# V loaded in two-token runs and put in order by TensorE, with merged final stores and new priorities, in a linear-attention and token-mixing kernel

## The chip, the cores and the metric

The kernel runs on one core of a Trainium2 chip. The metric is the device time of one execution in microseconds (us). Each comparison lists a median; the fast runs of one kernel are those within 1.5% of its fastest, and the others are called slow. Ratios are the mean time of one kernel's fast runs over that of the other's fast runs of the same rounds, so they are not quite the ratios of the medians.

The engines are TensorE (PE in the profile, its weight loads PEld), VectorE (DVE), ScalarE (ACT), GpSimd (POOL) and the sync engine (SP), which here only issues transfers. SPq is its queue.

## The reference

Four batch entries, 8 heads, 768 tokens, head width 48. First a recurrence per head, then a token mixer over the joined heads (384 columns):

```python
for t in range(S):
    cur = einsum('bhd,bhe->bhde', u * k_t, v_t)
    y[:, :, t] = einsum('bhd,bhde->bhe', r_t, state + cur)
    state = w_t[..., None] * state + einsum('bhd,bhe->bhde', k_t, v_t)
x = y joined over heads                                   # B, S, 384
wq, wk = x @ w_q, x @ w_k                                 # width 64
W_tok = scale * einsum('bsd,btd->bst', wq, wk)
out = relu(einsum('bst,btd->bsd', W_tok, x)) @ w_out
```

The recurrence runs in chunks of 128 tokens: decays become exponentials of summed logarithms, and each chunk needs a masked 128 by 128 product per head and one update of the state. Two chunks make a unit; there are 12 units, three to a batch entry. The token mixer of an entry can only end after its third unit, so its six stores come in a lump at each batch change.

## The kernel before

W, K and R are loaded with two neighbouring tokens on each partition, so a run in memory is 2 x 48 fp32 = 384 B. V is wanted in another order, the even tokens of a chunk on partitions 0 to 63 and the odd ones on 64 to 127, and it is loaded straight into that order, in four issues with runs of 192 B:

```python
def load(b, i, tl, ap):
    nc.sync.dma_start(out=view(tl, 0, [[D2, H], [1, D2]]),
        in_=ap[b, :, ds(i * U, U)].rearrange("h (p j) d -> p h (j d)", j=2))

def load_v(b, i, tl, c):                       # called for c = 0 and 1
    src = v[b, :, ds(i * U + c * C, C)].rearrange("h (q j) d -> j q h d", j=2)
    for j in range(2):
        nc.sync.dma_start(out=view(tl, c * DM, [[D, H], [1, D]], p0=64 * j, pn=64),
                          in_=src[j])
...
def f_vb():                                    # GpSimd, fp32 to bf16
    nc.gpsimd.tensor_copy(sb("VB", [C, 2 * DM]), vg)
...
def f_st(ii=ii, osb=osb, cs=cs):               # stores, two for each step
    dst = out[b, ds(ii * U, U)].rearrange("(c q j) d -> j q c d", j=2, q=64)
    for j in range(2):
        nc.sync.dma_start(out=dst[j][:, ds(cs[0], len(cs))], in_=view(osb, ...))
```

The order of instructions on each engine is fixed when the program is built. A small list scheduler takes the steps with their estimated lengths, a priority (`STEP * n + OFF[...]` for unit `n`) and the free buffers, and emits the steps in the order in which it would start them. Loads and stores share one queue, in that order; a store that waits for its data at the head of the queue holds all loads behind it. Inputs have three buffers each, and PSUM is handed out bank by bank.

## Time and profile before

| | before |
|---|---|
| the first three timed runs | 127.17, 127.18, 129.46 us |
| span of the profiled run (125.04 us) | 123.3 us |
| TensorE busy | 96.1 us, 78% |
| VectorE, GpSimd, ScalarE busy | 84.6, 77.4, 75.6 us |
| ScalarE's logarithm waiting for W | 10.1 us |

How to read the profile's lines: `wg`, `kg`, `rg` and `vg` are the buffers in which W, K, R and V land, `lw` is the logarithm, `os` the output buffer, `AM` a mask product; L374 is a line of the kernel. In rows of 40 digits the span is cut into 40 equal slices (numbered from 0), and a digit is the busy share of a slice in tenths, 9 being 90% or more. PEclk is the clock granted to TensorE, in tenths of full speed. DMA is the mean busy share of the 16 DMA engines; the windows give it as a fraction that can come out above 1.

The profile's row for that logarithm (busy us and mean ns of one, then the idle time of the engine before it and its cause):

```profile
L374 ACT ACTIVATE lw<-wg 128x768 bf16<-128x768 f32 x12 | 10.1, 844 | 10.1 <-DMA wg<-in_w_dram 10.1
```

Every unit starts with it: ScalarE waited 10.1 us in all for W to land.

### The profile page before, as it was taken

The page shows a single profiled execution, that of the slowest core. Times are in us where ns is not written, and L with a number is a line of the kernel's source. Part 1 is how long each engine was busy: PE and PEld are TensorE (multiplying, and loading weights), DVE is VectorE, ACT ScalarE, POOL GpSimd, SP SyncE. Part 2 cuts the span into 40 slices and gives each one's busy share as a digit, 9 for nine tenths or more (in the row PEclk, how much of TensorE's full clock was granted, in tenths as well). Part 3 has the DMA queues.
Part 4 walks back from the last instruction along what each step waited for, and adds up shares of the span by engine and source line. Part 5 has one row for each costly group of instructions (what it writes and reads, how often), then busy time and mean ns, then how long its engine had stood idle before and what let it go on. Part 6 is the DMA issues. An engine that isn't in the chain of part 4 may idle for free.

```text
span 123.3 us, 3766 instructions
## 1 busy us (share of the span) xinstructions
PE 96.1 (78%) x1528; PEld 71.7 (58%) x1528; DVE 84.6 (69%) x139; ACT 75.6 (61%) x105; POOL 77.4 (63%) x96
## 2 busy tenths in 40 slices
PE   0268986969699999679699998596999998969600
PEld 0256865847577678458477587484676885634300
DVE  6627969768685869682688998665975989634500
ACT  4362454659759958567667698487599894336100
POOL 6379699898895937943996848669945575200000
PEclk9999999999999999967999999999999999995875
DMA  3999989996999979999979688989899760000663
GB/s 67 307 224 312 189 255 299 203 308 125 266 227 229 275 167 254 262 227 222 275 159 312 117 223 241 297 155 312 177 273 248 197 196 0 0 0 5 158 152 73
DMA packets 67968, 24.62 MB, mean 200 GB/s; under 512 B 64496, under 2 KB 67952, under 8 KB 67952
## 3 DMA queue, kind: packets, MB, share of 16 engines
q1 hardware_dynamic: 67536, 24.39, 80.9%
q8 instruction: 12, 0.20, 0.6%
q10 hardware_dynamic: 416, 0.00, 0.2%
q14 instruction: 4, 0.03, 0.1%
HBM read 19.66 MB, written 4.72 MB: 198 GB/s over the span
## 4 chain that ended last, share of the span: by engine, by line
PE 33%; SPq 18%; ACT 14%; DMA 12%; POOL 9%; issue 6%; DVE 3%; ACTq 0%; POOLq 0%
PE PS L161 33%; POOL KT L447 8%; DMA wg<-in_w_dram 8%; SPq L197 7%; SPq L204 7%; ACT ep L406 5%; ACT en L400 5%; DMA vg<-in_v_dram 3%; SPq L718 2%; ACT lw L374 1%; ACT XT L297 1%; DVE os L301 1%; POOL ptm L453 1%; ACT QK L297 1%; SPq L727 1%
## 5 line engine op out<-in xcount | busy, mean ns | idle before, releaser
L496 DVE TENSOR_TENSOR AM<-PS,US 128x1024 bf16<-128x1024 f32 x24 | 28.8, 1218 | 3.4 <-PE PS L161 3.3
L447 POOL TENSOR_TENSOR KT<-ks,en 128x1024 bf16<-128x1024 bf16 (+1 forms) x13 | 23.7, 1824 | 4.6 <-DVE ks L425 2.4
L478 POOL TENSOR_TENSOR Vd<-VB,dd 128x768 bf16<-128x768 bf16 (+1 forms) x14 | 18.0, 1291 | 4.9 <-DVE dd L473 4.5
L400 ACT ACTIVATE en<-PS 128x1024 bf16<-128x1024 f32 (+1 forms) x14 | 12.6, 902 | 9.3 <-PE PS L161 7.2
L374 ACT ACTIVATE lw<-wg 128x768 bf16<-128x768 f32 x12 | 10.1, 844 | 10.1 <-DMA wg<-in_w_dram 10.1
L161 PE MATMUL PS<-CM,lw 64*128 64x128 bf16 x192 | 8.7, 240 | 7.5 <-ACT lw L374 7.3
L425 DVE COPY ks<-PS 128x1024 bf16<-128x1024 bf16 x12 | 8.3, 690 | 9.0 <-PE PS L161 9.0
L161 PE MATMUL PS<-wo,MX 128*128 128x384 bf16 x72 | 14.0, 356 | 0.2 <-ACT MX L307 0.2
L161 PEld LDWEIGHTS <-KT 48*128 48x128 bf16 (+1 forms) x272 | 10.6, 98 | 6.2 <-POOL KT L447 3.3
L297 ACT COPY XT<-PS 128x768 bf16<-128x768 bf16 (+1 forms) x12 | 9.2, 768 | 6.7 <-PE PS L161 6.7
L542 DVE TENSOR_TENSOR SB<-PS,ptm 128x384 bf16<-128x384 f32 x20 | 11.1, 553 | 2.7 <-PE PS L161 2.5
L406 ACT ACTIVATE ep<-PS 128x1024 bf16<-128x1024 f32 (+1 forms) x14 | 12.9, 919 | 0.0
L381 POOL CAST k<-kg 128x768 bf16<-128x768 f32 x12 | 9.9, 822 | 4.3 <-DMA kg<-in_k_dram 4.2
L381 POOL CAST r<-rg 128x768 bf16<-128x768 f32 x12 | 9.9, 826 | 3.8 <-DMA rg<-in_r_dram 3.8
L461 POOL CAST VB<-vg 128x768 bf16<-128x768 f32 x12 | 9.9, 824 | 3.7 <-PE PS L161 3.7
L299 ACT ACTIVATE X<-PS,gx 128x768 bf16<-128x768 f32 (+1 forms) x11 | 9.6, 870 | 4.0 <-PE PS L161 3.1
L161 PEld LDWEIGHTS <-lw 64*128 64x128 bf16 x192 | 6.5, 105 | 8.7 <-ACT lw L374 7.7
L436 DVE TENSOR_TENSOR RT<-PS,ep 128x1024 bf16<-128x1024 bf16 (+1 forms) x14 | 8.5, 612 | 3.5 <-PE PS L161 3.5
L161 PEld LDWEIGHTS <-MX 128*128 128x128 bf16 x72 | 7.3, 105 | 5.7 <-issue 1.6
L161 PE MATMUL PS<-RT,KT 48*128 48x128 bf16 x192 | 8.8, 225 | 1.6 <-POOL KT L447 1.0
L161 PEld LDWEIGHTS <-AM 128*128 128x128 bf16 x192 | 8.7, 99 | 2.0 <-issue 0.3
L301 DVE COPY os<-PS 128x768 f32<-128x768 f32 (+1 forms) x7 | 5.5, 786 | 5.6 <-PE PS L161 4.0
(70 smaller groups left out, 197.1 us busy)
## 6 DMA issues: line engine op xcount, KB each, us to landing
wg<-in_w_dram SPq DMA_DIRECT2D x12, 384.0 KB, 4.1
kg<-in_k_dram SPq DMA_DIRECT2D x12, 384.0 KB, 5.1
rg<-in_r_dram SPq DMA_DIRECT2D x12, 384.0 KB, 6.1
vg<-in_v_dram SPq DMA_DIRECT2D x48, 96.0 KB, 4.0
out_dram<-os SPq DMA_DIRECT2D x18, 192.0 KB, 3.0
out_dram<-os SPq DMA_DIRECT2D x12, 96.0 KB, 2.2
wof<-in_moe_w_out_dram SPq DMA_DIRECT2D x1, 576.0 KB, 4.9
wqf<-in_moe_w_q_dram SPq DMA_DIRECT2D x1, 96.0 KB, 4.0
```

Source lines behind the costliest of these rows:

```text
L161: nc.tensor.matmul(o, l, rr, start=start, stop=stop, skip_group_check=True, is_transpose=trans)
L297: nc.scalar.copy(o, i)
L299: nc.scalar.activation(o, i, ACT.Copy, bias=0.0, scale=by)
L374: nc.scalar.activation(view(lw, 0, [[64, H], [512, 2], [1, D]]), view(wg, 0, [[D2, H], [D, 2], [1, D]]), ACT.Ln, bias=0.0, scale=math.exp( ...
L381: nc.gpsimd.tensor_copy(view(dst, 0, [[64, H], [512, 2], [1, D]]), view(src, 0, [[D2, H], [D, 2], [1, D]]))
L400: nc.scalar.activation(sb("en", [C, 1024])[:, cols(cs, 512)], t["cw"][:, cols(cs, 512)], ACT.Exp, bias=0.0, scale=-1.0)
L406: nc.scalar.activation(view(ep, cs[0] * NP * EW + 66, [[EW, NP * len(cs)], [-65, 2], [1, 64]]), t["cw"][:, cols(cs, 512)], ACT.Exp, bias=0 ...
L447: e.tensor_tensor(sb("KT", [C, 1024])[:, cols(cs, 512)], t["ks"][:, cols(cs, 512)], t["en"][:, cols(cs, 512)], ALU.mult)
L461: nc.gpsimd.tensor_copy(sb("VB", [C, 2 * DM]), vg)
L478: nc.gpsimd.tensor_tensor(sb("Vd", [C, 2 * DM])[:, cols(cs, DM)], t["VB"][:, cols(cs, DM)], view(t["dd"], cs[0] * H, [[1, len(cs) * H], [0 ...
L496: nc.vector.tensor_tensor(view(sb(f"AM{c}", [C, 1024]), 0, [[C, 8], [1, C]]), view(t[f"A{c}"], 0, [[C, 8], [1, C]]), view(US, 0, [[0, 8], ...
L542: nc.vector.tensor_tensor(view(x, 0, [[D, H], [1, D]]), view(t[f"sn{c}"], 0, [[D, H], [1, D]]), view(t["ptm"], c * 8, [[1, 8], [0, D]]), A ...
```

## The change

The intent is fewer and longer transfers. V is loaded like K, in one issue of 384 B runs. GpSimd casts it, TensorE puts the tokens in order by products with a 0/1 selection matrix, and ScalarE or VectorE copies the result out of PSUM. Merged final stores and new priorities come with it. The core of the diff, shortened:

```diff
+    PM = const([C, 2 * C], BF16, "PM")                    # 0/1, built at the start
-    OFF = dict(load=-4, ln=207, c16=-50, ...)
-    ENG = dict(KT="PPPPPPPPPPDP", kd="DDADADDADDAD", ...)
+    OFF = dict(load=-38, ln=232, c16=-17, ..., v16=-147, vp=-43, vb=-59, ...)
+    ENG = dict(KT="PPPPPPPPPDPP", vb="AAAADAADAAAA", kd="DDADDAADADAA", ...)
...                                                         # and new cost estimates
-        add("SP", 2150, "load", f_lv, fill="vg", ...)       # 4 issues
+        add("SP", 1500, "load", lambda: load(b, i, vg, v), fill="vg", ...)
...
-            nc.gpsimd.tensor_copy(sb("VB", [C, 2 * DM]), vg)
+            nc.gpsimd.tensor_copy(view(v16, 0, [[D, H], [DM, 2], [1, D]]),
+                                  view(vg, 0, [[D2, H], [D, 2], [1, D]]))
+        def f_vp():
+            t["vp"] = x = wtile("vp")                       # two PSUM banks
+            for j in range(2):
+                for c in range(2):
+                    mm(x[:, ds(c * 512, DM)], PM[ds(c * 64, 64), ds(j * C, C)],
+                       v16[ds(c * 64, 64), ds(j * DM, DM)], start=(j == 0), stop=(j == 1))
+        def f_vb():
+            copy(vbe, VB, vp)                               # ScalarE 10x, VectorE 2x
...
-  last batch: f_st for each half unit, two issues of 96 KB each, all on sync (12)
+  last batch: f_st for each unit, two issues of 192 KB (6), the very last on ScalarE's queue
...
+  the last token sum's copies wait for all of its groups, not for the last alone
```

More of the change, by code (lines that the diff above doesn't have):

```diff
@@ L199, in load @@
             in_=ap[b, :, ds(i * U, U)].rearrange("h (p j) d -> p h (j d)", j=2))
-    def load_v(b, i, tl, c):
-        src = v[b, :, ds(i * U + c * C, C)].rearrange("h (q j) d -> j q h d", j=2)
-        for j in range(2):
-            nc.sync.dma_start(out=view(tl, c * DM, [[D, H], [1, D]], p0=64 * j, pn=64),
-                              in_=src[j])
     ID16 = const([C, C], BF16, "ID16")
@@ L225 @@
     nc.vector.memset(ID16, 0.0)
+    nc.vector.memset(PM, 0.0)
     for t in LW:
@@ L247 @@
                                     fill=0.0, base=-j, channel_multiplier=-2)
+    for c in range(2):
+        for j in range(2):
+            m = PM[ds(c * 64, 64), ds(j * C + j * 64, 64)]
+            nc.gpsimd.affine_select(m, m, pattern=[[1, 64]], compare_op=ALU.not_equal,
+                                    fill=1.0, base=0, channel_multiplier=-1)
     nc.gpsimd.affine_select(ID16, ID16, pattern=[[1, C]], compare_op=ALU.not_equal, fill=1.0,
@@ L258 @@
     STEP = 100
-    OFF = dict(load=-4, ln=207, c16=-50, cw=60, ex=34, rT=123, ks=-72, qT=284, RT=139, KT=27,
-               ptm=275, vb=34, dps=61, vd=-63, A=8, am=115, kb=94, kd=-148, sn=-109, sb=184,
-               y=108, x=-84, xt=129, xts=-98, qk=64, qks=249, T=148, mx=-51, rl=317, fp=103,
-               os=13, st=149)
-    ENG = dict(KT="PPPPPPPPPPDP", kd="DDADADDADDAD", xts="AAAAAAAAAAAD", x="AAADAAAAAAAA",
-               qks="DAAAAAAAAADA", rl="AAAADAAAAAAA", os="AADDDAADADAD")
+    OFF = dict(load=-38, ln=232, c16=-17, cw=-165, ex=-1247, rT=520, ks=698, qT=-1585, RT=735,
+               KT=49, ptm=-98, v16=-147, vp=-43, vb=-59, dps=288, vd=-159, A=-391, am=545,
+               kb=332, kd=-769, sn=-476, sb=170, y=86, x=-436, xt=541, xts=-163, qk=811,
+               qks=-869, T=612, mx=226, rl=-553, fp=-948, os=1147, st=189)
+    ENG = dict(KT="PPPPPPPPPDPP", vb="AAAADAADAAAA", kd="DDADDAADADAA", xts="DADAAAADDDAA",
+               x="AAAAAAAAAAAA", qks="DAADAAADAADA", rl="DDDAAAAAAAAA", os="AAADAAAADAAD")
     SPLIT = (0, B * NU - 1)
@@ L272 @@
         kinds[name] = 2
-    for name in ("en", "ks", "qT", "RT", "KT", "ptm", "VB", "dd", "Vd", "AM0", "AM1", "KD", "XT"):
+    for name in ("en", "ks", "qT", "RT", "KT", "ptm", "v16", "VB", "dd", "Vd", "AM0", "AM1", "KD", "XT"):
         kinds[name] = NS
@@ L290, in took @@
         if eng == "P":
-            return 60 + int(cols * 1.87)
-        return 110 + int(cols * (0.52 if half else 1.04))
+            return 100 + int(cols * 1.93)
+        return 150 + int(cols * (0.52 if half else 1.04))
     def copy(eng, o, i, by=None):
@@ L360, in cols @@
             return ds(cs[0] * w_, len(cs) * w_)
-        g = {x: Got() for x in ("wg kg rg vg lw k16 r16 cw ep en kT rT ks qT RT KT ptm VB dps dd Vd"
+        g = {x: Got() for x in ("wg kg rg vg lw k16 r16 v16 vp cw ep en kT rT ks qT RT KT ptm VB dps dd Vd"
                                 " A0 A1 AM0 AM1 kb KD sn y xt XT qk").split()}
-        add("SP", 1460, "load", lambda: load(b, i, wg, w), fill="wg", got=g["wg"], lag=2000)
-        add("SP", 1460, "load", lambda: load(b, i, kg, k), fill="kg", got=g["kg"], lag=2000)
-        add("SP", 1460, "load", lambda: load(b, i, rg, r), fill="rg", got=g["rg"], lag=2000)
-        def f_lv():
-            load_v(b, i, vg, 0)
-            load_v(b, i, vg, 1)
-        add("SP", 2150, "load", f_lv, fill="vg", got=g["vg"], lag=2000)
+        add("SP", 1500, "load", lambda: load(b, i, wg, w), fill="wg", got=g["wg"], lag=2000)
+        add("SP", 1500, "load", lambda: load(b, i, kg, k), fill="kg", got=g["kg"], lag=2000)
+        add("SP", 1500, "load", lambda: load(b, i, rg, r), fill="rg", got=g["rg"], lag=2000)
+        add("SP", 1500, "load", lambda: load(b, i, vg, v), fill="vg", got=g["vg"], lag=2000)
         def f_ln():
@@ L425, in f_ks @@
             nc.vector.tensor_copy(sb("ks", [C, 1024]), t["kT"])
-        add("D", 640, "ks", f_ks, fill="ks", got=g["ks"], use=[g["kT"]])
+        add("D", 670, "ks", f_ks, fill="ks", got=g["ks"], use=[g["kT"]])
         def f_qT():
             nc.vector.tensor_tensor(sb("qT", [C, 1024]), t["rT"], t["ks"], ALU.mult)
-        add("D", 640, "qT", f_qT, fill="qT", got=g["qT"], use=[g["rT"], g["ks"]])
+        add("D", 670, "qT", f_qT, fill="qT", got=g["qT"], use=[g["rT"], g["ks"]])
         for cs in fine:
@@ L458, in unit, with f_v16 @@
                 use=[g["ep"]])
+        def f_v16():
+            nc.gpsimd.tensor_copy(view(sb("v16", [C, 2 * DM]), 0, [[D, H], [DM, 2], [1, D]]),
+                                  view(vg, 0, [[D2, H], [D, 2], [1, D]]))
+        add("P", 830, "v16", f_v16, fill="v16", got=g["v16"], use=[g["vg"]])
+        def f_vp():
+            t["vp"] = x = wtile("vp")
+            for j in range(2):
+                for c in range(2):
+                    mm(x[:, ds(c * 512, DM)], PM[ds(c * 64, 64), ds(j * C, C)],
+                       t["v16"][ds(c * 64, 64), ds(j * DM, DM)], start=(j == 0), stop=(j == 1))
+        add("PE", 370, "vp", f_vp, fill="w", got=g["vp"], use=[g["v16"]])
+        vbe = ENG["vb"][n]
         def f_vb():
-            nc.gpsimd.tensor_copy(sb("VB", [C, 2 * DM]), vg)
-        add("P", 830, "vb", f_vb, fill="VB", got=g["VB"], use=[g["vg"]])
+            copy(vbe, view(sb("VB", [C, 2 * DM]), 0, [[DM, 2], [1, DM]]),
+                 view(t["vp"], 0, [[512, 2], [1, DM]]))
+        add(vbe, took(vbe, 2 * DM), "vb", f_vb, fill="VB", got=g["VB"], use=[g["vp"]])
         def f_dps():
@@ L499, in f_am @@
                     view(US, 0, [[0, 8], [1, C]]), ALU.mult)
-            add("D", 1180, "am", f_am, more=2 * c, fill=f"AM{c}", got=g[f"AM{c}"], cs=(c,),
+            add("D", 1200, "am", f_am, more=2 * c, fill=f"AM{c}", got=g[f"AM{c}"], cs=(c,),
                 use=[g[f"A{c}"]])
@@ L544, in f_sb @@
                                             view(t["ptm"], c * 8, [[1, 8], [0, D]]), ALU.mult)
-                st_ = add("D", 510, "sb", f_sb, more=2 * c, fill="SB", cs=(c,), use=[gsn, g["ptm"]])
+                st_ = add("D", 540, "sb", f_sb, more=2 * c, fill="SB", cs=(c,), use=[gsn, g["ptm"]])
                 new.put(st_, (0, 1))
@@ L646, in unit @@
         groups = [[0, 1, 2, 3], [4], [5]] if end else [list(range(NCH))]
+        Tall = []
         for gs in groups:
-            T_ = add("PE", 165 * len(gs), "T", f_T(gs),
+            Tall.append(add("PE", 165 * len(gs), "T", f_T(gs),
                      [batch["qks"][x] for x in gs] + [batch["xs"][x] for x in gs]
                      + ([gT.first] if gT.first else []),
-                     more=OFF["am"] - OFF["T"] if end and gs[0] == 0 else 0, fill="s", got=gT)
+                     more=OFF["am"] - OFF["T"] if end and gs[0] == 0 else 0, fill="s", got=gT))
         def f_Ts(c):
@@ L662, in f_Ts @@
             return f
-        Ts = [add("AD"[c], took("AD"[c], DM), "T", f_Ts(c), [T_], more=1, use=[gT])
+        Ts = [add("AD"[c], took("AD"[c], DM), "T", f_Ts(c), Tall, more=1, use=[gT])
               for c in range(2 if end else 1)]
@@ L713, in unit, with f_st, f @@
                     use=[gf])
-                def f_st(ii=ii, osb=osb, cs=cs):
+            def f_st(j, e, ii=ii, osb=osb):
+                def f():
                     dst = out[b, ds(ii * U, U)].rearrange("(c q j) d -> j q c d", j=2, q=64)
-                    for j in range(2):
-                        nc.sync.dma_start(
-                            out=dst[j][:, ds(cs[0], len(cs))],
-                            in_=view(osb, cs[0] * DM, [[DM, len(cs)], [1, DM]], p0=64 * j, pn=64))
-                add("SP", 560 * len(cs), "st", f_st, more=6 * ii, cs=cs, use=[go], lag=2000)
+                    e.dma_start(out=dst[j],
+                                in_=view(osb, 0, [[DM, 2], [1, DM]], p0=64 * j, pn=64))
+                return f
+            add("SP", 620, "st", f_st(0, nc.sync), more=6 * ii, use=[go], lag=2000)
+            if end and ii == NU - 1:
+                add("A", 500, "st", f_st(1, nc.scalar), more=6 * ii, use=[go], lag=2000)
+            else:
+                add("SP", 620, "st", f_st(1, nc.sync), more=6 * ii, use=[go], lag=2000)
     state = {}
```

## The prediction

> **What bounds the kernel now.** I read the page first (busy shares and the slices), then the chain of waits, then the sync queue's own order of issues, then windows over whole batches. A "unit" below is 256 tokens of one batch entry; there are 12 units, three to a batch.
>
> From the page:
>
> ```profile
> PE 96.1 (78%) x1528; PEld 71.7 (58%) x1528; DVE 84.6 (69%) x139; ACT 75.6 (61%) x105; POOL 77.4 (63%) x96
> PE   0268986969699999679699998596999998969600
> PEclk9999999999999999967999999999999999995875
> DMA  3999989996999979999979688989899760000663
> vg<-in_v_dram SPq DMA_DIRECT2D x48, 96.0 KB, 4.0
> ```
>
> No engine is full, TensorE is the fullest, and the DMA row is near 9 until the loads end at about 98 us. The TensorE row has holes near slices 16 to 18 and 25, one in each middle batch change. The sync queue (SP issues all loads and stores) over one batch:
>
> ```profile
> 36.42 0.57 SPq L197 DMA_DIRECT2D wg<-in_w_dram  x1
> 37.09 0.61 SPq L197 DMA_DIRECT2D kg<-in_k_dram  x1
> 37.79 0.67 SPq L197 DMA_DIRECT2D rg<-in_r_dram  x1
> 38.56 4.11 SPq L204 DMA_DIRECT2D vg<-in_v_dram  x4
> 43.20 4.42 SPq L718 DMA_DIRECT2D out_dram<-os  x6
> 47.66 0.61 SPq L197 DMA_DIRECT2D wg<-in_w_dram  x1
> ```
>
> Columns are start and length in us. V takes as long to issue (4.11 us for four) as W, K and R and their waits together, and the six stores of a batch then hold the next W back. The chain that ended last shows what that does:
>
> ```profile
> 46.57 0.40 SPq L718
> 46.97 0.04 issue
> 47.01 0.61 SPq L718
> 47.62 0.04 issue
> 47.66 5.29 DMA wg<-in_w_dram
> ...
> 53.03 0.85 ACT lw L374
> 53.89 0.05 issue
> 53.93 1.05 PE PS L161 x16
> ```
>
> W is issued late, needs 5.29 us to land in a full DMA stream, and only then the logarithm and the decay products start. What TensorE did meanwhile, and the batches as a whole (busy us and instruction counts per engine, then granted clock, DMA share, GB/s):
>
> ```profile
> 50.00:51.50 1.50, 0.30 (x9) 0.21 (x6) 0.85 (x3) 0.89 (x2) 1.50 (x3) 1.00 1.03 279
> 53.50:57.00 3.50, 3.07 (x41) 2.42 (x41) 1.49 (x2) 2.98 (x4) 1.65 (x2) 0.51 0.88 173
> 22.10:47.70 25.60, 22.86 (x397) 17.25 (x392) 18.93 (x28) 19.41 (x25) 20.70 (x22) 1.00 0.96 225
> 47.70:73.90 26.20, 22.83 (x382) 17.50 (x380) 19.90 (x29) 18.06 (x23) 17.93 (x18) 0.93 0.93 227
> 73.90:100.10 26.20, 22.88 (x404) 17.51 (x399) 19.18 (x29) 20.48 (x28) 17.57 (x20) 1.00 0.96 241
> ```
>
> The starved stretch leaves TensorE at half clock for 3.5 us. A batch takes 25.6 to 26.2 us, and that is what one batch of issues takes too (22.1 to 47.66 on the queue). So I read: the load stream (issue, DMA rate, stores in the same queue) and TensorE at 87% are almost equally tight; the stream sets the hand-overs between batches.
>
> The end is a third stage, bound by store issue:
>
> ```profile
> 112.97 7.56 SPq L718 DMA_DIRECT2D out_dram<-os  x12
> ```
>
> The last copy out ends at 116.8 us, yet the queue goes on issuing until 120.5.
>
> **What the Trainium skill says.** "DMA: Bandwidth & Descriptors", Specifications, gives 512 B as the least transfer for line rate. All inputs here are below it: 384 B for W, K, R (two tokens), 192 B for V (one token). The trace agrees that shorter is worse: 322 GB/s from 9.5 to 11.5 us, where mostly W, K and R land, against 192 GB/s from 22.0 to 23.5, where mostly V lands, with the DMA share over 1 in both. The same page, "Issuing engines are not separate DMA queues", says that a second issuing engine saves only the sequencer's issue time; an issue is about 0.6 us here. "TensorE: Matmul & The Clock Gate", What's actually happening, says that the array's clock halves after idle and is released by sustained work: the 0.51 above agrees. "PSUM — Partial Sum Buffer", Specifications, says that GpSimd has no access to PSUM; that is why V's evacuation must go to ScalarE or VectorE. In the trace GpSimd reads only SBUF.
>
> **The change, part by part.**
>
> *V loads.* 48 issues of 96 KB become 12 of 384 KB, with half the packets. Queue: four issues take 3.2 to 4.7 us, one should take 0.6 to 1.3 like the load of R, so 2.5 us less per unit and 7.5 per batch: the queue's 25.6 us fall to about 18. DMA: 393 KB at 192 GB/s is 2.05 us, at 322 it is 1.22, so 0.83 us per unit, 10 us in all. Neither is a saving by itself; it stops being the bound. At the start it is a saving: the second unit's W was issued at 6.40 us and should come at about 3.9.
>
> *Selection products.* Four matmuls per unit of 384 columns. Eighteen such in the dense stretch at 92.8 us took 3.09 us, 0.17 each, so 0.69 us in a row. They contract 64 rows and alternate between the two halves, as the decay products do: 16 of those take 0.62 us, no more than 8 full-height transposes (0.61). So 0.35 to 0.7 us per unit, 4 to 8 us of TensorE in all, 1 to 2 us per batch.
>
> *Evacuation.* GpSimd's cast (0.82 us) stays as a rearranging cast, like K's at 0.82: nothing. New is a PSUM copy of 768 columns, 10 times on ScalarE (0.80 us, from its copies of that size) and twice on VectorE (0.96). With the re-dealt engines my count for ScalarE is +8.0 (V) +0.9 (X) -3.2 (XT) -1.0 (QK) -1.6 (MX) +1.6 (os) +0.9 (KD) = +5.6, to 81 us. VectorE is +1.9 -1.0 +2.3 +1.1 +1.9 -1.9 -0.7 = +3.6, to 88 us; here XT at 0.56 is interpolated between 358 ns for 384 and 690 ns for 1024 columns. GpSimd gets four more mask instructions at the start, about 1 us, ended before K lands. None of these becomes the bound: 88 us in 12 units is 7.4 us per unit against a pace of 8.7.
>
> *The batches.* What remains is TensorE. In its one full stretch, 40 to 50 us, it did 171 matmuls in 10 us. The three batches from 22.1 to 100.1 us hold 397+382+404 = 1183, and 36 come in: 1219/17.1 = 71.3 us against 78. I do not believe in a full engine for that long; at 96% of this rate it is 74.2 us. **Gain about 3.8 us**, the new products paid.
>
> *The start.* **Gain about 2.2 us**, the 2.5 of the earlier W less some loss in the longer way of V (cast, product, copy: two more hand-overs).
>
> *The end.* Twelve stores become six, one of them on ScalarE's queue. The last pair waits for the copy at 116.8; ahead of it on SP the middle pair starts at 115.8 and ends at 117.1, so the last SP issue starts at 117.1 instead of 119.9. A 192 KB store lands in 3.0 us, a 96 KB one in 2.2: 120.1 instead of 122.1. **Gain 2.0 us.** The ordered token sums change dependences only: nothing.
>
> Sum: 2.2 + 3.8 + 2.0 = 8.0 us, 127.2 to 119.2. I round up to 120.0 because the middle term needs a good order of instructions that I have not seen.
>
> **Rivals.** *TensorE takes over at once*: if its holes are dependences (the chain of X, KT and qT waits is 7.4 us of its idle time between 10 and 110 us, the decay logarithm only 2.1) rather than loads, the middle gains nothing and pays 4 us for the products: 127.2 - 2.2 - 2.0 + 4 = 127. For it: 90 to 100 us is 98% busy with no help from loads. Against it: the two worst holes, around 50 and 79 us, both wait for W. *PSUM becomes the bound*: a new two-bank tile lives through product and copy, some 2 us per unit, on eight banks that the mask tiles already crowd. It would show as products waiting for evacuations; middle gain halved, about 122. *The stream was the whole bound*: then batches drop to what VectorE needs, about 22 us plus bubbles, and the total goes to 115 or 116. Against it: TensorE would have to be full throughout.
>
> **Range and chances.** Start and end (4.2 us) are nearly arithmetic; the middle runs from -4 to +8. Low 115.5, high 125.0. To be within 2% the gain would have to be below 2.5 us, which needs the first rival nearly whole: 15%. Slower by 2% needs a bad order besides: 3%. Faster: 82%.
>
> **What would show it.** V's row with 12 issues and the DMA row down to 7 or 8 with gaps; second W at about 4 us; no half-clock stretch near 54 us; batches of 24 to 25 us with TensorE over 93% busy; DMA waits of the logarithm below 6 us instead of 10.1; last SP store about 2 us nearer to the last copy. I am wrong if TensorE's idle time stays as it is, its releasers now being V's copy or evacuations of PSUM, or if the half-clock stretch comes back elsewhere.

## The result, and the profile after

119.77 us median of four runs (118.32 to 119.94), beside 128.32 us for the kernel before in the same rounds; the ratio of the fast runs is 0.9393, with a 95% interval of 0.9269 to 0.9516. A second comparison on another chip gave 119.87 us and a ratio of 0.9613 (0.9575 to 0.9651). The kernel after hardly moved between the two; the fast runs of the kernel before did, so the two comparisons put the gain at 4 and 6%.

The page of the kernel after:

```profile
PE 98.2 (83%) x1576; PEld 71.8 (61%) x1576; DVE 87.3 (74%) x146; ACT 78.5 (66%) x111; POOL 77.5 (66%) x100
PE   0159996798899999999999999898999999969600
PEclk9999999999999999999999999999999999995996
DMA  2999999999998916989999997999500007250193
L372 ACT ACTIVATE lw<-wg 128x768 bf16<-128x768 f32 x12 | 10.3, 854 | 3.3 <-DMA wg<-in_w_dram 3.3
vg<-in_v_dram SPq DMA_DIRECT2D x12, 384.0 KB, 5.2
```

TensorE's row is 8 or 9 from slice 8 to slice 34, the half-clock stretch in the middle is gone, the transfers fall quiet from slice 29 on instead of 33, and the logarithm waits 3.3 us for W instead of 10.1. The sync queue at the first batch change, columns as before:

```profile
34.75 1.06 SPq L197 DMA_DIRECT2D wg<-in_w_dram  x1
35.90 1.10 SPq L197 DMA_DIRECT2D kg<-in_k_dram  x1
37.09 1.94 SPq L197 DMA_DIRECT2D rg<-in_r_dram  x1
43.48 1.37 SPq L733 DMA_DIRECT2D out_dram<-os  x2
44.94 0.55 SPq L197 DMA_DIRECT2D vg<-in_v_dram  x1
46.09 2.74 SPq L733 DMA_DIRECT2D out_dram<-os  x4
48.88 0.87 SPq L197 DMA_DIRECT2D wg<-in_w_dram  x1
```

These six stores are those of the first batch entry; the loads run ahead of the compute, so the next W in the queue is already that of unit 6, the first of the third entry. It goes out at 34.75 us, not at 47.66. Two things differ. The earlier loads are through sooner, and W, K and R now stand *ahead* of the six stores in the queue. The prediction saw the first and not the second. A single issue of W or K also grew, from about 0.6 to 1.1 us. At the start of the kernel after, the queue goes at the pace of the transfers: four loads of 393 KB go out between 4.43 and 9.29 us, which is 324 GB/s, and that window moves 322 GB/s. Why an issue takes as long near 35 us, where 232 GB/s move, is not shown.

The chain that ended last, by engine, before:

```profile
PE 33%; SPq 18%; ACT 14%; DMA 12%; POOL 9%; issue 6%; DVE 3%; ACTq 0%; POOLq 0%
```

and after:

```profile
PE 62%; DVE 9%; POOL 8%; ACT 7%; issue 5%; DMA 3%; DVEq 0%; ACTq 0%
```

The queue and the transfers made 30% of the chain, now 3%; TensorE's own work has taken their place.

The second half of the run in windows (columns as in the prediction), before and then after:

```profile
50.00:100.00 50.00, 43.31 (x732) 32.96 (x729) 36.75 (x54) 36.50 (x49) 33.98 (x35) 0.97 0.95 233
```

```profile
50.00:100.00 50.00, 48.66 (x860) 36.94 (x860) 41.78 (x63) 41.29 (x58) 36.06 (x37) 1.00 0.74 198
```

The same 50 us hold 860 matmuls instead of 732, at 97% busy instead of 87%, and the DMA share has room.

To see where the time came from, I took from VectorE's timelines the end of the second mask product of a unit, one of the last things that a unit needs:

| us | before | after | change in this stage |
|---|---|---|---|
| unit 0 masked | 14.54 | 15.57 | +1.03 |
| unit 4 masked | 48.33 | 48.95 | -0.41 |
| unit 11 masked | 104.83 | 99.90 | -5.55 |
| last copy out ends | 116.80 | 111.88 | +0.01 |
| end of the span | 123.3 | 118.1 | -0.28 |

So in these two profiled runs all of the gain (5.2 us) lies between the first batch change and the last unit. The first 48 us gained nothing, and the stage after the last copy 0.3 us. By the medians of the first rounds the gain is 8.6 us; the profiled run of before was one of its fastest, so these two traces do not show where the rest lies.

### The profile page after: what moved, and what is told of

Read it like the earlier page. It is cut to its first block, busy times and chain, and to the rows that moved or that the text cites. A ratio compares the mean times of both kernels' runs of the same rounds, so it can differ in the third digit from the quotient of the medians.

```text
span 118.1 us, 3867 instructions
## 1 busy us (share of the span) xinstructions
PE 98.2 (83%) x1576; PEld 71.8 (61%) x1576; DVE 87.3 (74%) x146; ACT 78.5 (66%) x111; POOL 77.5 (66%) x100
## 4 chain that ended last, share of the span: by engine, by line
PE 62%; DVE 9%; POOL 8%; ACT 7%; issue 5%; DMA 3%; DVEq 0%; ACTq 0%
PE PS L161 62%; POOL KT L445 3%; DMA wg<-in_w_dram 3%; DVE qT L427 2%; ACT en L398 2%; DVE AM L510 2%; ACT ep L404 2%; POOL r L379 2%; POOL v L459 1%; DVE RT L434 1%; DVE MX L310 1%; ACT lw L372 1%; ACT XT L298 1%; DVE ks L423 1%; DVE KD L304 1%
## 5 line engine op out<-in xcount | busy, mean ns | idle before, releaser
L300 ACT ACTIVATE X<-PS,gx 128x768 bf16<-128x768 f32 (+1 forms) x12 | 10.5, 878 | 6.2 <-PE PS L161 6.1
L459 POOL CAST v<-vg 128x768 bf16<-128x768 f32 x12 | 9.9, 824 | 3.5 <-DMA vg<-in_v_dram 3.5
L427 DVE TENSOR_TENSOR qT<-PS,ks 128x1024 bf16<-128x1024 bf16 x12 | 8.3, 688 | 3.9 <-PE PS L161 3.8
L161 PE MATMUL PS<-RT,KT 48*128 48x128 bf16 x192 | 9.3, 222 | 1.8 <-POOL KT L445 1.6
L161 PEld LDWEIGHTS <-AM 128*128 128x128 bf16 x192 | 8.2, 96 | 2.7 <-issue 0.8
L298 ACT CAST VB<-PS 128x768 bf16<-128x768 f32 x10 | 8.0, 802 | 2.7 <-PE PS L161 2.4
L298 ACT COPY os<-PS 128x768 f32<-128x768 f32 (+1 forms) x10 | 6.9, 706 | 4.3 <-PE PS L161 4.1
```

Of the source, the lines that this page charges most:

```text
L161: nc.tensor.matmul(o, l, rr, start=start, stop=stop, skip_group_check=True, is_transpose=trans)
L298: nc.scalar.copy(o, i)
L427: nc.vector.tensor_tensor(sb("qT", [C, 1024]), t["rT"], t["ks"], ALU.mult)
L459: nc.gpsimd.tensor_copy(view(sb("v16", [C, 2 * DM]), 0, [[D, H], [DM, 2], [1, D]]), view(vg, 0, [[D2, H], [D, 2], [1, D]]))
```

## The experiments

The theory to begin with was that of the prediction: the stream of loads (four issues and short packets for V) made W late. The rivals were the new order of instructions and the merged stores. Wherever "compute order unchanged" is said, a listing of both programs showed the same instructions in the same order on all compute engines, apart from the named edit and queue issues.

### Faster V loads alone

```diff
-            load_v(b, i, vg, 0)
-            load_v(b, i, vg, 1)
+            load(b, i, vg, v)
-            nc.gpsimd.tensor_copy(VB, vg)
+            nc.gpsimd.tensor_copy(VB, view(vg, 0, [[D2, H], [D, 2], [1, D]]))   # wrong token order
```

> The kernel before with V loaded in two-token runs, one issue of 384 KB, and cast straight from there: tokens in the wrong order, so the result is wrong on purpose; every other engine has the same instructions in the same order. Theory (the load stream made the late W at the batch changes): the hole of TensorE near 53 us and its half-clock stretch go, 3 to 5 us faster than before, a ratio of 0.96 to 0.975. Rival (the new order of instructions made the gain): under 1 us, ratio above 0.99.

Measured: 125.76 us median against 127.52, ratio 0.9991 (0.9845 to 1.0137); the result was wrong, as intended. **The theory fell.** The queue of this run (what I read here is the order, which is fixed) shows why:

```profile
32.72 1.10 SPq L197 DMA_DIRECT2D vg<-in_v_dram  x1
43.67 4.07 SPq L718 DMA_DIRECT2D out_dram<-os  x6
47.78 0.60 SPq L197 DMA_DIRECT2D wg<-in_w_dram  x1
```

V of unit 5 is issued 5.8 us earlier than before (38.56), and then the queue stands still for 10 us, because the next thing in it is the six stores, whose data is not ready. W of unit 6 goes out at 47.78, as before. A faster stream is only a longer wait in front of the stores.

### The new order of instructions alone

```diff
 (kernel before)
-    OFF = dict(load=-4, ln=207, ...)      ENG = dict(KT="PPPPPPPPPPDP", ...)
+    OFF = dict(load=-38, ln=232, ...)     ENG = dict(KT="PPPPPPPPPDPP", ...)
-            return 60 + int(cols * 1.87)   # and 110 + ... for VectorE
+            return 100 + int(cols * 1.93)  # and 150 + ... for VectorE
```

> The kernel before with only the new priorities, deal of engines and cost figures. Theory: the loads stay as slow, so at most 1 us faster, and perhaps slower as these priorities were found for another program: ratio 0.99 to 1.03. Rival (new order): 3 to 5 us faster, ratio 0.96 to 0.975.

Measured: 130.01 us against 127.52, ratio 1.0279 (0.9954 to 1.0604). So the order alone does not help either; the logarithm's wait for W is 14.0 us here, more than before. W and K of unit 6 already go out ahead of the stores in this run (42.41 and 43.08 us, the first stores at 46.56), and the logarithm of unit 6 waits for nothing; the waits have moved to other units. So the place of the stores, with slow loads and this order, does not make the kernel faster by itself.

### The merged final stores alone

```diff
 (kernel before, the store step)
+                    if end and cs == (0,):
+                        return
                     for j in range(2):
-                        nc.sync.dma_start(out=dst[j][:, ds(cs[0], len(cs))], in_=...)
+                        e = nc.scalar if end and ii == NU - 1 and j == 1 else nc.sync
+                        e.dma_start(out=dst[j], in_=view(osb, 0, [[DM, 2], [1, DM]], ...))
```

> The kernel before with only the last batch's stores merged to six, the last one on ScalarE's queue; all compute engines unchanged. The prediction said 2.0 us faster (ratio 0.984). The two traces say about 0.5 us: last data landed 4.9 us after the last copy before and 4.4 after (ratio 0.993 to 0.998).

Measured: 127.34 us (124.96 to 128.27) against 127.52 (125.23 to 129.63); only one of its four runs was a fast one, so there is no ratio. Inconclusive at this size; the end is tested again on the kernel after, which spreads less.

### The new V path with the old order

```diff
 (kernel after)
-    OFF, ENG and cost figures of after
+    those of before, with v16=33, vp=34 beside the old vb=34, and vb="AAAADAADAAAA"
```

> The kernel after with the old priorities, deal of engines and cost figures, and the three new steps of V put next to the old cast's priority. Theory: most of the gain stays, ratio to before 0.95 to 0.975, 1 to 4 us slower than after. Rival (new order): the gain is gone, ratio 0.99 or more, since the products are extra work.

Measured: 131.69 us against 127.52, ratio 1.0341 (1.0 to 1.0683). Only two of its four runs were fast ones, and the profile is of a slow one. There W was no longer late (its logarithm waited 3.4 us for it), and still the kernel was slower than before. So neither half of the change gained anything without the other, with the places that I gave to the three new steps. This run does not say which of the old priorities does the harm.

### The stores behind the next loads

The first run pointed to the queue. The next edit leaves the programs of all compute engines as they are and only moves the six stores of the first and of the second batch behind W, K and R of the next unit:

```diff
 (kernel before, where the steps are emitted)
         for s in plan.order():
+            if is_store(s) and s["n"] < plan.last_store:    # batches 0 and 1
+                held.append(s); since = 0
+                continue
             s["fn"]()
+            if held and s["eng"] == "SP":
+                since += 1
+                if since == 3:
+                    emit all of held; held = []
```

> The kernel before, every compute engine unchanged, only the sync queue reordered: the six stores of the first and second batch go behind W, K and R of the next unit instead of ahead of them. Faster loads alone gave nothing (their fast run sat with the stores at the head of the queue from 32.7 to 43.7 us and issued the next W at 47.8, as before). New theory (the place of the stores in the queue makes W late): the holes at 50 to 54 and 77 to 80 us shrink, 1 to 4 us faster, ratio 0.97 to 0.99; less than the next run, as the slow V stream reaches the stores late. Rival (TensorE's other dependences set the pace, the holes only absorb slack): under 1 us.

Measured: 123.45 us against 127.64, ratio 0.9715 (0.9647 to 0.9782). A change of the sync queue alone, with V's short packets and four issues left as they were, is worth 2.9%. The queue at the first batch change:

```profile
43.55 1.13 SPq L197 DMA_DIRECT2D wg<-in_w_dram  x1
46.74 4.77 SPq L719 DMA_DIRECT2D out_dram<-os  x6
```

The logarithm's total wait for W hardly fell (9.4 us, 10.1 before). What changed is where it waits: no longer at units 6 and 9, the first of the third and fourth entries, where it waited 2.14 and 1.76 us before, but at unit 10 and longer at units 2 and 3.

### Both

The edits of the first and of the last experiment together.

> The same reordered queue together with V in two-token runs (wrong token order, wrong result on purpose), old compute order, no products. New theory: both parts are needed, 3 to 6 us faster than before, ratio 0.955 to 0.975, the first loads of a batch landing before the stores. Rival (only a new order of the compute engines can use earlier loads): under 1 us, ratio above 0.99.

Measured: 122.57 us against 127.64, ratio 0.9641 (0.9587 to 0.9694), with the compute order of *before* and no products. W of unit 6 in the five traces (the first column from the sync queue, the second from ScalarE's timeline):

| | W of unit 6 issued, us | its logarithm starts, us | ratio to before |
|---|---|---|---|
| before | 47.66 | 53.03 | 1 |
| faster V, old queue | 47.78 | 54.41 | 0.9991 |
| V as before, queue moved | 43.55 | 51.20 | 0.9715 |
| faster V, queue moved | 34.86 | 50.90 | 0.9641 |
| after | 34.75 | 43.35 | 0.9393 and 0.9613 |

With the stores out of the way the logarithm of unit 6 starts about 2 us earlier, with or without faster V, though W is issued 8.7 us earlier with it. ScalarE's timeline shows why: the logarithm follows the step before it (a copy that ends at 51.30 and 51.00 us) without a gap and waits for W in neither run. V as before, then faster V:

```profile
51.20 0.83 ACT L375 ACTIVATE lw<-wg 128x768 bf16<-128x768 f32 x1
```

```profile
50.90 0.83 ACT L374 ACTIVATE lw<-wg 128x768 bf16<-128x768 f32 x1
```

Where faster V does show is unit 10: with V as before its logarithm still waits 1.80 us for W and starts at 84.59 us, with faster V it waits for nothing and starts at 82.41. The total wait for W fell to 3.5 us, near that of after (3.3). Nor does an early logarithm set the pace by itself: after has it at 43.35 us, 7.5 us earlier than this run, and yet unit 6 is masked at 61.55 us, no sooner than here (61.41; 63.54 before).

### The kernel after with short packets

```diff
 (kernel after)
-    VG: 8 x 96 columns;     one issue, (j d) together: 384 B packets
+    VG: 8 x 2 x 64 columns; two issues, token j to place j * 64: 192 B packets
```

> The kernel after with V's packets at 192 B again (the two tokens of a partition go to places 64 apart, two issues of 192 KB); compute order unchanged, result right. If the short packets were what held before: 3 to 6 us slower than after, ratio to before 0.965 to 1.0. If the place of the loads in the queue and the compute order matter more: at most 2 us slower than after, ratio to before under 0.955.

Measured: 125.46 us against 127.64, ratio 0.9853 (0.9789 to 0.9916), so 5.6 us slower than the 119.87 us of after by the medians (119.77 and 119.87 on two chips, this run on a third), and 2.5 to 4.9% slower by the two ratios of after to before. Compute order unchanged. The row of the logarithm is back to waiting:

```profile
L377 ACT ACTIVATE lw<-wg 128x768 bf16<-128x768 f32 x12 | 10.1, 845 | 17.6 <-DMA wg<-in_w_dram 13.0
```

So even with the queue in the good order, V in short packets takes back more than half of the gain. The profile of this run fell in the slow state; its median is over all runs, its ratio over the four fast ones. It also issues V 24 times instead of 12, which this run does not separate from the length of the packets.

### The selection products twice

```diff
 (kernel after)
-            for j in range(2):
+            for j in (0, 1, 0, 1):       # the second pass starts the sum anew
```

> The kernel after with the selection products made twice (the second pass starts the sum anew, so the result is right): 48 more matmuls of 384 columns, nothing else moved. The prediction priced the products at 4 to 8 us of TensorE, with TensorE the bound: so 4 to 6 us slower than after, ratio to before 0.97 to 0.99. If they sit in TensorE's idle time or overlap: under 2 us slower, ratio under 0.955.

Measured: 122.15 us against 127.64, ratio 0.9635 (0.9572 to 0.9699); by the medians 2.3 us slower than after, on another chip; the ratios to before give anything from 0.2 to 2.6%. The traces side with the median: unit 11 is masked at 103.04 us here and at 100.39 in the copy of after below. The row of the products in the kernel after, then in this run:

```profile
L161 PE MATMUL PS<-v,PM 64*128 64x384 bf16 x48 | 6.3, 342 | 0.5 <-DVE AM L510 0.4
L161 PE MATMUL PS<-v,PM 64*128 64x384 bf16 x96 | 10.5, 340 | 0.5 <-DVE AM L510 0.4
```

So the second pass made TensorE busy for 4.2 us more, and the kernel slower by about half of that. TensorE is close to being the bound, not wholly. If a first pass costs what a second does, the products cost 2 to 3 us.

### The kernel after again

An unchanged copy, to have after beside the last runs.

> The kernel after unchanged, beside the others on the same chip, as its first ratio (0.9393) has an interval of 2.5%. Expected 0.935 to 0.945.

Measured: 119.87 us against 126.08, ratio 0.9613 (0.9575 to 0.9651). The expectation was missed, and the reason is the denominator: five of the eleven runs of before were between 124.07 and 125.01 us here.

### The end: old stores in the kernel after

```diff
 (kernel after, last batch)
-  two issues of 192 KB for each unit, the very last on ScalarE's queue
+  two issues of 96 KB for each copy, twelve in all, all on sync
```

> The kernel after with the last batch's stores as before: twelve of 96 KB, all on the sync queue; the order of the compute engines unchanged. Theory from the traces (the end is worth 0.5 us, since the merged stores start later and land later): 0 to 1 us slower than after, and the last SP issue some 2 us later than now. The prediction: 2.0 us slower. Before alone with merged stores gave nothing clear of noise.

Measured: 121.04 us, ratio 0.9688 (0.9642 to 0.9734), beside 0.9613 for after: 1.2 us slower by the medians. The last stores in the queue, first here:

```profile
109.07 8.26 SPq L733 DMA_DIRECT2D out_dram<-os  x12
```

and in the copy of after:

```profile
110.61 3.30 SPq L733 DMA_DIRECT2D out_dram<-os  x5
```

The last copy out ends at 113.06 us here and at 112.72 there. The queue is through 4.3 us after it (109.07 + 8.26 = 117.33), and 1.2 us after it (113.91) with merged stores. That is 3.1 us less issue, and only 1.2 us less time. The merged stores start 1.5 us later, since a pair of copies must be ready, and then all are in flight together: the DMA share in the first profile of after stands at 0.95 to 1.06 from 112.0 to 115.5 us, and a store of 192 KB lands in 2.9 us against 2.2 us for 96 KB. The last one, on ScalarE's queue, landed 4.1 us after its issue, that of the first profile of after 3.4 us:

```profile
out_dram<-os ACTq DMA_DIRECT2D x1, 192.0 KB, 3.4
```

### The end: half stores on three queues

```diff
 (kernel after, last batch, for each copy)
+   96 KB of partitions 0-63   on sync
+   96 KB of partitions 64-127 on GpSimd's queue; of the last unit on ScalarE's
```

> The kernel after with half-size stores in the last batch as each copy ends, spread over three queues: one half of the partitions on sync, the other on GpSimd's queue and for the last pair on ScalarE's. If the end waits for pairs of copies and for issue: last data 1.5 to 2 us sooner, 1 to 2 us faster than after, ratio 0.925 to 0.935. If it waits for the DMA rate of 1.2 MB: no gain.

Measured: 117.70 us, ratio 0.9434 (0.9393 to 0.9474), so 2.2 us faster than after by the medians and faster than both kernels. Its sync queue:

```profile
108.08 4.25 SPq L733 DMA_DIRECT2D out_dram<-os  x6
```

In its profile 5.3 us pass from the end of the last copy (110.57) to the end of the span (115.9), against 6.2 us in the first profile of after and 5.6 us in that of its copy, which ran in the same rounds (112.72 to 118.3). So the stores account for 0.3 to 0.9 us of the gain. The larger part, 1.3 or 2.1 us, comes before the last copy. There TensorE's clock differs: between 106.0 and 109.5 us it was 0.52 in the first profile of after, with 26 matmuls, and 1.00 here, with 34. The last 18 products, in the copy of after and then here:

```profile
107.35 4.78 PE L161 MATMUL PS<-wo,MX 128*128 128x384 bf16 x18 [0.20 <-ACT MX L308]
```

```profile
106.87 3.10 PE L161 MATMUL PS<-wo,MX 128*128 128x384 bf16 x18 [0.20 <-ACT MX L308]
```

In the copy the clock was 0.50 from 108 to 111 us. The stretch before is as thinly filled in both, and I have not shown why the clock stayed up, nor that the stores had a part in it. It was no single run: all six lie between 117.27 and 118.30 us, with a mean granted clock of 0.973 to 0.995 against 0.966 to 0.980 for the copy of after.

### The weights' casts on ScalarE too

The first 48 us gained nothing although loads came earlier, and GpSimd is 92 to 100% busy between 10 and 30 us in the kernel after. So I moved the three casts of the mixer's weights (2.3 us) to ScalarE, behind the third logarithm, all else as in the last run:

```diff
-        nc.gpsimd.tensor_scalar_mul(wq_sb, wq_f, scale)     # and two copies
+        nc.scalar.activation(wq_sb, wq_f, ACT.Copy, bias=0.0, scale=scale)
```

> As the last one, and the three casts of the MLP weights (2.3 us of GpSimd near 19 us, where GpSimd is at 92 to 100% busy) moved to ScalarE, which is half idle there; the order of everything else kept. If GpSimd bounds the first stage: 1 to 2 us faster than the last one, ratio 0.91 to 0.925, and the third unit's casts about 2 us sooner. If not: within 0.5 us of the last one.

Measured: 117.35 us, ratio 0.9409 (0.938 to 0.9438), 0.35 us below the last run by the medians, with the intervals overlapping. The masks of unit 2 end at 29.64 us instead of 29.97. GpSimd's third pair of casts did start 2.0 us sooner (20.40 instead of 22.42), and its next product then waited 1.29 us for VectorE. So GpSimd alone doesn't bound the start; what does stays open. This is the fastest version by its median, with correct results.

## Why the prediction was right or wrong

The predicted time was 120.0 us and 119.77 were measured, inside the range. That the sum came out is partly luck. In the profiled pair the gain is 5.2 us and not 8.0: nothing at the start, more than predicted in the middle, less at the end. But the sum started from 127.2 us, and the profiled run of before took 125.04; this difference, and the 0.8 us by which the sum was rounded up, hide the error.

- **The bound.** "The stream sets the hand-overs between batches" was right as to the place. The mechanism was half right. The lines that I quoted show the stores in front of W, but I made the stream's length the cause and took for granted that a shorter queue brings W forward. The run with faster V alone shows that it does not (ratio 0.9991, 0.9845 to 1.0137): with the old queue order the stores' place decides, and the faster stream counts only once W is ahead of them. I had not asked where the new order puts the stores. Two readings were wrong besides. V's issue (4.11 us) does not take as long as those of W, K and R but about twice as long (36.42 to 38.56, 2.1 us). And that a batch takes as long as its issues was no evidence, since I had cut the windows at the queue's own issues of W (22.10, 47.66, 73.90); by the ends of the mask products of units 2, 5, 8 and 11 the batches took 24.7, 26.4 and 23.9 us.
- **The batches, 3.8 us.** This term was too small: the profiled runs show 5.5 us, from the first batch change to the last unit, the products paid. Their price of 4 to 8 us of TensorE holds as busy time (6.3 us in their row, 4.2 us more for a second pass); in the kernel's time a second pass cost 2.3 us by the medians. The loads on the other engines came out below the count: ScalarE 78.5 us (81 predicted), VectorE 87.3 (88).
- **The start, 2.2 us.** This step failed. W of the second unit was issued at 4.43 us instead of 6.40 (3.9 predicted), and its logarithm started at 9.41 instead of 10.56; but the masks of units 0 to 4 ended 0.1 to 1.0 us later, not 2.2 us earlier. An earlier load was not what these units waited for.
- **The end, 2.0 us.** The mechanism was right and its size was off: 1.2 us by the run with the old stores, 0.3 us between the two first profiles. The issue saved was even more than the 2.8 us that I had counted (3.1), but I set the landing of a merged store at 3.0 us. The last one, on ScalarE's queue, took 4.1 us in the copy of after (3.4 in the first profile), with the merged stores coming in one burst.
- **The rivals.** TensorE did come close to the bound: 97% busy in the second half, and extra products cost time. That PSUM would be the bound did not show: in the profile of after no wait of TensorE for a step that reads PSUM exceeds 0.6 us in total.
- **The signs named.** V's issues (12), the second W at about 4 us, the logarithm's wait (3.3 us, under the 6 named), no half clock near 54 us and TensorE over 93% (97% from 50 to 100 us) all came. The DMA row did not go down to 7 or 8: it stays at 9 while loads run, with gaps, and ends earlier. The batches took 27.1, 17.7 and 25.2 us by the masks, so 23.3 in the mean where 24 to 25 was said, but not one of them in that range. The last SP store came 1.2 us nearer to the last copy (from 3.7 to 2.5 us after it) in the first profile of after, and 2.5 us nearer in its copy, where 2 us was said.

What stays open: what the ordered token sums do by themselves, which no run changed alone; why the first 48 us take as long with loads that come earlier, why the old priorities with the new V path are slower than both (1.0341), what the new order adds once the stores are moved, and the clock of the last 10 us.

## What to carry to other kernels

A transfer's place in its queue can matter more than its speed: before shortening a load stream, look at what stands at the head of the queue when the stream has caught up, and put stores that wait for late results behind the loads that the next stage starts with. Here the stores' place alone gave 2.9%, faster loads alone nothing that shows, and the two together 3.6%. The new V path and the new priorities gained nothing one without the other, so find priorities for the program that results. At the end of a kernel, count the issues that stand between the last result and the last store: twelve in one queue went on for 4.3 us after the last copy, and fewer stores, or the same ones spread over three queues, shortened that. Which of the two is better is not settled here, as most of what the spread stores gained lies with the clock.

## What the Trainium skill lacked or had wrong

- "DMA: Bandwidth & Descriptors", Issuing engines are not separate DMA queues: it says that issue time is usually small relative to the transfer. At the end of this kernel an issue of a 96 KB store took 0.59 us, beside 2.2 us from issue to landing, and twelve of them kept one queue for 8.26 us, waits for copies included; spread over three queues, the sync queue's half took 4.25 us, and the profiles show 5.3 us instead of 6.9 from the end of the last copy to the end of the span (115.9 - 110.57 and 120.0 - 113.06).
- The same page, Anatomy of one DMA, says that semaphore waits happen on the issuing sequencer. It does not say what follows for a queue shared by loads and stores: in the run with faster V alone a store waiting at the head held the loads behind it back for 10 us (32.72 + 1.10 to 43.67 us). In the kernel before, moving the stores behind the next loads was worth 2.9%.
- "DMA: Bandwidth & Descriptors", Specifications, gives 512 B as the least size for line rate but no rate below it (a later section, Why small descriptors are slow, gives an overhead per packet, not a rate for such loads). In two short windows of the kernel before the loads ran at 322 GB/s with mostly 384 B packets and at 192 GB/s with mostly 192 B packets; going back to 192 B for V alone, with twice its issues, cost 5.6 us by the medians.
- I found no page that gives the length of a local load's issue when the DMA engines are full: W's median issue grew from 0.62 to 1.08 us in the kernel after.
